# Two scatters a head, squares ahead of rectifications, norms a block later, transposes later, in a fused attention and expert kernel

## The chip, the cores and the metric

The kernel runs on one core of a Trainium2 chip. The metric is the device time of one execution in microseconds (us); the kernel before takes 831.98 us, the median of three runs (830.75 to 832.9).

## What is computed

The reference has two halves, and the second reads what the first wrote.

```python
def _attn_ref(q, k, v, s):            # q, k, v: 8 batches, 8 heads, 576 rows, 64 columns
    scores = scale * np.matmul(q, k.transpose(0, 1, 3, 2))
    bias = -(cum[:, :, :, None] - cum[:, :, None, :])        # cum = cumsum(max(s, 0))
    scores = np.where(causal, -1000000000.0, scores + np.minimum(bias, 0.0))
    attn = softmax(scores)
    return np.matmul(attn, v)
def _moe_ref(x, expert_emb, tau, w1, w2):                    # x: 4608 rows of 512
    logits = normalized(x) @ normalized(expert_emb).T / tau
    expert_idx = np.argmax(logits, axis=1)                   # one of 8 experts a row
    for e in range(E):
        h = np.maximum(x[mask] @ w1[e], 0.0)                 # 512 to 1024
        out[mask] = gate_w[mask, None] * (h @ w2[e])         # 1024 to 512
```

(`softmax` and `normalized` stand for the lines that spell them out.)

## The kernel before

**Attention.** There are 64 heads. `step(n)` (lines 859 to 987) is one step of a software pipeline: for head n the score matmuls and exponentials, for head n - 2 the product with v (`pv`, lines 464 to 482, into the one PSUM tile `om`), for head n - 3 the normalization (`norm1` to `norm3`, VectorE, lines 484 to 510), which writes 72 columns of the row tile `xt` of its batch. `om` must have been read by `norm3` (line 505) before the next `pv` may begin. `pl_` (line 457) makes the low half of the exponentials' split, as a subtraction on GpSimd, or on VectorE.

When the eighth head of a batch is normalized, its 576 rows are routed (`router`): an expert for each row and a place in it. Five scatters of 128 rows (`scat`, line 616, an indirect DMA from GpSimd's queue) then write the rows to `xs` in DRAM, ordered by expert. There are two `xt` tiles, so that the first `norm3` of a batch has to wait until the scatters of the batch two before it have read theirs. How many scatters a step issues is set by `SCN` (line 31), a number for each of a batch's eight heads, up to head 41; from head 42 on (`n < NH - 22` false) it is one a step, and five from head 59 on.

**Experts.** The rows of each expert are gathered back, 128 at a time (`xload`, line 675, at most CAP = 640 rows, so tiles t = 0 to 4). `xprep` transposes them on TensorE (line 700, into a PSUM tile, of which the kind `pxm` exists once and the kind `pxs` twice), copies them as 16 bit values to `xH` (ScalarE, line 705) and the remainder to `xL` (VectorE, line 707); `xstat` squares them (ScalarE, line 689) and sums the expert's logits (VectorE). `l1(m, e, lo, hi)` is block m of eight of the first matrix product (line 788; 12 matmuls where the columns fit in one PSUM bank, else 24), ended by a rectification on ScalarE (line 797, tiles `hv`, `hp`, `hq`) and a subtraction on VectorE (line 798). `l2(e, t)` is the second product for one tile (24 matmuls, line 806), ended by a scaling on VectorE (line 811, into `Kx`) and a scatter to `out` (line 812). Expert 0 is begun with its first SPL = 384 rows while batch 7 is still being routed; tiles 3 and 4 follow.

**Weights.** They come as 32 bit values, 256 KB at a time, into a ring. `wsq` squares them (ScalarE, line 740) and, at the eighth piece, casts the sums (line 742). `wnorm` sums over partitions with a small matmul into `om` (line 751) and makes a power of two of it (VectorE, lines 752 to 758). `wcv` scales and casts a piece (ScalarE, line 768), `wlow` makes its low half (VectorE, line 776) and starts the next load. The first eight pieces lie in tiles that are used again later: `hv` is written over the raw pieces in `vh`, which the `wlow` of those pieces must have read.

All engines run their own queue in the order in which the code issues instructions (`manual_schedule`); nothing reorders them.

Of the kernel before, what the change touches and what calls it, by code (L numbers as in the profile page):

```python
# [31 lines left out]
SCN = [1, 1, 0, 0, 0, 0, 2, 1]  # L32
# [11 lines left out]
SPL = 384  # L44
# [59 lines left out]
def main(ctx, tc, qkh, qkc, vtin, s_in, emb, tau, w1h, w2h, out, shared, nb):  # L104
# [668 lines left out]
    def wlow():  # L773
        while lows:
            q, l, a, s, h = lows.popleft()
            nc.vector.scalar_tensor_tensor(l, a, s, h, op0=ALU.mult, op1=ALU.subtract)  # L776
            wissue(q + 15)
# [19 lines left out]
        nc.scalar.activation(hH, hp, AF.Relu)  # L797
        nc.vector.scalar_tensor_tensor(hL, hp, 0.0, hH, op0=ALU.max, op1=ALU.subtract)  # L798

    def l2(e, t, mid=None):  # L800
        y = pxs()
        for m in range(8):
            wH, wL = wt(2, m)
            hH, hL = htile(m)
            for k, (h, w) in enumerate(((hH, wH), (hL, wH), (hH, wL))):
                nc.tensor.matmul(y, h[:, 128 * t:128 * t + 128], w, start=(m == 0 and k == 0), stop=(m == 7 and k == 2))  # L806
            if m == 3 and mid:
                mid()
        xf = X[("i", e, t)]
        ys = HT["Kx"][:, t % 3]  # L810
        nc.vector.tensor_scalar(ys, y, xf[3], IX["RS"][:, 2 * e + 1:2 * e + 2], op0=ALU.mult, op1=ALU.mult)  # L811
        nc.gpsimd.indirect_dma_start(out=out, out_offset=bass.IndirectOffsetOnAxis(ap=xf[0].bitcast(U32), axis=0),  # L812
                                     in_=ys, in_offset=None, bounds_check=NT - 1, oob_is_err=False)
# [45 lines left out]
    def step(n):  # L859
# [63 lines left out]
        s3(m)  # L923
        if n < 0:
            heat(1)
        wlow()
        if live:
            tbl(n)
        mslot()
        if prev and PS(n) < 1600:  # L930
            pl_(n - 1, PS(n), 1600, "v")
        if n == 1:
            vscale(0)
            fslot()
            while tasks:
                slot()
            emm(0)
            vcp(0, False)
            vcp(0, True)
# [21 lines left out]
        if live:  # L961
            prep(n, False)
            if n:
                vcp(n, True)
        k = n - NH + 8
        if k > 0:
            wsq((0, 2, 3, 6, 8, 8, 9, 10, 12, 14, 16)[k])
            wcv((0, 0, 0, 0, 0, 1, 2, 2, 1, 2, 0)[k], True)
# [7 lines left out]
            loadt(b1, c8)  # L976
        if n == NH - 8:
            wissue(3)
        for _ in range(SCN[c8] if n < NH - 22 else 1 + 4 * (n > NH - 6)):
            scatter()  # L980
        later()
        if live and c == (n < HG):
# [7 lines left out]
    def PS(n):  # L990
        return 1600 if n < NH - 6 else 1024
# [48 lines left out]
    for n in range(1 - LA, NH + 3):  # L1040
        step(n)
    for m in range(3, 8):
        l1(m, 0, 0, SPL, partial(some, 12) if m == 5 else None)
        if m == 3:
            wlow()
            some(12)
            wnorm()
        if m > 3:
            wcv((2, 1, 2, 2)[m - 4])
        if 3 < m < 7:  # L1050
            xstat(0, m - 4)
        if m > 5:
            some(0)
        if m == 7:
            for f in X[("g", 0, 0)][0:2]:
                f()
# [9 lines left out]
        for f in X[("g", 0, 0)][2:4]:  # L1066
            f()

    def second():
        for t in range(SPL // 128, NTL):  # L1070
            xprep(0, t, (pxm, pxs)[t % 2]())
        for t in range(2):
            xload(1, t)
        xprep(1, 2, pxm())

    wsq(18)
    l2(0, 0, opening)
    wsq(21)
    l2(0, 1)
    wsq(24)  # L1080
    l2(0, 2, second)
    for e in range(NE):
        nx = e + 1 < NE
        w2, w1 = 16 * e + 8, 16 * e + 16
        for m in range(8):
            l1(m, e, 0 if e else SPL, CAP)
            if e == 1:
                wsq(w2 + (6, 8)[m] if m < 2 else w1 + (0, 0, 0, 1, 4, 7)[m - 2])
                wcv((2, 0, 2, 2, 2, 2, 0, 0)[m])
                if m == 1:  # L1090
                    wnorm()
            elif e > 1:
                if m < 4:
                    wcv(2)
                elif nx:
                    wsq(w1 + 2 * (m - 3))
            if nx and e > 0 and m == 1:
                xinfo(e + 1, 0, NTL)
            if nx and e > 0 and m == 2:
                for t in range(3):  # L1100
                    xload(e + 1, t)
            if e == 0 and m in (2, 5):
                xprep(1, m // 3, (pxm, pxs)[m // 3]())
                xload(1, 3 + m // 3)
            if e == 0 and m % 2:
                X[("g", 0, SPL // 128)][m // 2]()
            if e > 0 and m < 4:
                X[("g", e, 0)][m]()
            if e == 1 and m == 4:
                count()  # L1110
        for t in range(0 if e else SPL // 128, NTL):
            if nx:
                xprep(e + 1, t, (pxs if e == 0 and t == 3 else pxm)())
                if e and t + 3 < NTL:
                    xload(e + 1, t + 3)
                if e == 0:
                    if t == 3:
                        wnorm()
                    wcv(3)
                    wsq(24 + 2 * (t - 2))  # L1120
                else:
                    if t == 0 and e == 1:
                        wsq(w1 + 8)
                    if t == 1:
                        wnorm()
                    if t:
                        wcv(2)
                    wsq(w2 + 16 + min(8, 2 * t + 2))
                    if t == 4:
                        wnorm()  # L1130
            l2(e, t)

# [120 lines left out]
```

## Time and profile before

| | us |
|---|---|
| median of three runs | 831.98 |
| lowest, highest | 830.75, 832.9 |
| the profiled execution, its own time | 830.1 |
| its span, first to last instruction | 828.3 |
| TensorE busy in the span | 784.2 |
| VectorE, ScalarE, GpSimd busy | 527.5, 570.7, 380.0 |
| mean granted clock of TensorE | 0.979 |

Attention fills the first 370 us of the span, the passage to the experts lies between 330 and 450 us, and the experts fill the rest. Busy shares are averages over all of it. In the rows PE is TensorE's matmuls, PEld its weight loads, DVE VectorE, ACT ScalarE, POOL GpSimd and SP SyncE; a name such as L788 is the line of the kernel.

### The profile page before, as it was taken

Reading aid. Unit: us, or ns where it says so; the run is one execution under the profiler, and the core shown is the slowest. Engines: PE = TensorE matmul, PEld = TensorE weight load, DVE = VectorE, ACT = ScalarE, POOL = GpSimd, SP = SyncE. Lnnn points to the kernel's source line nnn. Section 1 sums busy time; section 2 is a strip of 40 time slices with the busy share of each in tenths; the row PEclk is TensorE's granted clock in tenths of the full one; section 3 lists DMA queues with packets and bytes.
Section 4 is the critical chain, followed back from the end, with each engine's and each line's share of the span. In section 5 each row is a group of like instructions: output and inputs, shape, how many; then the busy total and the mean of one; then the engine's idle time right before and its main releaser. Section 6 shows DMA issues by size and latency. Waiting matters only on the chain. (4 is left out here: it accounts for less than half of the span.)

```text
span 828.3 us, 19525 instructions
## 1 busy us (share of the span) xinstructions
PE 784.2 (95%) x7394; PEld 590.5 (71%) x7394; DVE 527.5 (64%) x1782; ACT 570.7 (69%) x1009; POOL 380.0 (46%) x369
## 2 busy tenths in 40 slices
PE   7699999999999999888898999999999999999992
PEld 3599999999999999874565557466575565655741
DVE  7667888887878777687366555564554556645510
ACT  6589999898989898677355846746557467475400
POOL 8758798989798888552321230221111302211011
PEclk9899999999999999999999999999999999999997
DMA  8977879797979886744333343442553424521010
GB/s 159 204 163 138 184 172 202 178 200 180 201 180 196 185 184 140 230 145 163 110 119 120 123 142 120 140 155 68 155 157 106 143 85 144 179 67 56 1 39 27
DMA packets 44256, 117.17 MB, mean 141 GB/s; under 512 B 6320, under 2 KB 6724, under 8 KB 43294
## 3 DMA queue, kind: packets, MB, share of 16 engines
q0 software_dynamic: 20240, 70.92, 36.6%
q1 hardware_dynamic: 23920, 44.97, 18.1%
q8 instruction: 59, 0.97, 0.5%
q14 instruction: 37, 0.30, 0.1%
HBM read 95.23 MB, written 21.49 MB: 141 GB/s over the span
## 5 line engine op out<-in xcount | busy, mean ns | idle before, releaser
L232 POOL TENSOR_TENSOR PL<-P 128x576 f16<-128x576 f32 (+2 forms) x128 | 202.1, 1673 | 25.8 <-ACT P L452 14.2
L788 PEld LDWEIGHTS <-wt 128*128 128x128 f16 x1536 | 150.3, 98 | 64.4 <-issue 4.2
L788 PE MATMUL h<-xH,wt 128*128 128x320 f16 (+2 forms) x1024 | 188.5, 301 | 0.5 <-DVE hq L798 0.5
L812 POOL DMA_INDIRECT out<-Kx,xj x40 | 39.7, 994 | 182.5 <-DVE Kx L811 178.7
L348 DVE CUSTOM_DVE_ANT_0 junk<-s,mS 128x192 bf16<-128x192 f32 (+3 forms) x256 | 102.1, 420 | 21.4 <-PE s L340 16.8
L480 PE MATMUL om<-vh,P 128*128 128x73 f16 x960 | 110.6, 200 | 4.9 <-DVE xt L505 4.5
L481 PE MATMUL om<-vl,P 128*128 128x72 f16 x960 | 110.1, 198 | 0.0
L482 PE MATMUL om<-vh,PL 128*128 128x73 f16 x960 | 110.0, 199 | 0.0
L679 POOL DMA_INDIRECT Qx<-xs,idx x40 | 42.5, 1062 | 146.3 <-ACT vjunk L689 124.0
L788 PE MATMUL h<-xL,wt 128*128 128x320 f16 (+1 forms) x480 | 106.9, 299 | 0.0
L481 PEld LDWEIGHTS <-P 128*128 128x128 bf16 x960 | 95.2, 99 | 7.3 <-issue 5.8
L340 PE MATMUL s<-qkb 96*128 96x288 f32 (+4 forms) x384 | 95.8, 333 | 3.8 <-DMA qkb<-P 2.7
L806 PE MATMUL pxs<-wt,hp 128*128 128x512 f16 x360 | 97.3, 379 | 0.0
L482 PEld LDWEIGHTS <-PL 128*128 128x128 f16 x960 | 94.4, 98 | 0.0
L480 PEld LDWEIGHTS <-P 128*128 128x128 bf16 x960 | 94.1, 99 | 0.2
L806 PE MATMUL pxs<-wt,hq 128*128 128x512 f16 x360 | 92.0, 383 | 0.0
L811 DVE TENSOR_SCALAR Kx<-pxs,xj,idx 128x512 f32<-128x512 f32 x40 | 32.4, 810 | 81.3 <-PE pxs L806 81.2
L340 PEld LDWEIGHTS s<-qkb 96*128 96x128 f32 x384 | 66.2, 198 | 9.3 <-issue 3.2
L455 ACT ACTIVATE P<-tb 128x1024 f32<-128x1024 f32 x64 | 65.5, 1023 | 7.2 <-PE tb L423 3.6
L806 PEld LDWEIGHTS <-hq 128*128 128x128 f16 x360 | 35.5, 99 | 43.0 <-issue 1.1
L806 PEld LDWEIGHTS <-hp 128*128 128x128 f16 x360 | 35.2, 98 | 42.8 <-issue 0.5
L806 PE MATMUL pxs<-wt,hv 128*128 128x512 f16 x240 | 64.0, 379 | 0.3 <-DVE wt L776 0.3
(223 smaller groups left out, 1722.6 us busy)
## 6 DMA issues: line engine op xcount, KB each, us to landing
qkb<-qkh POOLq DMA_DIRECT2D x15, 1216.0 KB, 9.5
ring<-w2h SPq DMA_DIRECT2D x44, 256.0 KB
ring<-w1h SPq DMA_DIRECT2D x36, 256.0 KB
vT<-vtin SPq DMA_DIRECT2D x28, 320.0 KB
KC<-qkh POOLq DMA_DIRECT2D x15, 576.0 KB, 8.7
QC<-qkh POOLq DMA_DIRECT2D x15, 576.0 KB, 7.7
rw<-w1h SPq DMA_DIRECT2D x15, 256.0 KB
rw<-w2h SPq DMA_DIRECT2D x12, 256.0 KB
```

The lines of the kernel that those rows point to most:

```text
L232: nc.gpsimd.tensor_tensor(out, a, b_, op=ALU.subtract)
L340: nc.tensor.matmul(out, G[g]["QB"][0:96, h, 128 * i:128 * i + 128], G[g]["KB"][0:96, h, lo:hi], start=True, stop=True)
L348: nc.vector.tensor_tensor_reduce(out=jk, in0=src, in1=ms, scale=1.0, scalar=NEG, op0=ALU.add, op1=ALU.max, accum_out=MP[n // 2][:, n % 2, ...
L455: nc.scalar.activation(HD[n]["P32"][:, 576:1600], HD[n]["tb"], AF.Exp, scale=0.125)
L480: nc.tensor.matmul(out, lh, vh[:, kb], start=(kb == 0), stop=False)
L481: nc.tensor.matmul(out[:, u:u + 72], lh, vl[:, kb], start=False, stop=False)
L482: nc.tensor.matmul(out, ll, vh[:, kb], start=False, stop=(kb == j))
L679: ins = nc.gpsimd.indirect_dma_start(out=x.bitcast(I32), out_offset=None, in_=src, in_offset=bass.IndirectOffsetOnAxis(ap=X[("i", e, t)][1 ...
L788: nc.tensor.matmul(h[:, u, 0:b - a], w[:, 128 * c:128 * c + 128], x[:, c, lo + a:lo + b], start=(c == 0 and k == 0), stop=(c == 3 and k == 2))
L806: nc.tensor.matmul(y, h[:, 128 * t:128 * t + 128], w, start=(m == 0 and k == 0), stop=(m == 7 and k == 2))
L811: nc.vector.tensor_scalar(ys, y, xf[3], IX["RS"][:, 2 * e + 1:2 * e + 2], op0=ALU.mult, op1=ALU.mult)
L812: nc.gpsimd.indirect_dma_start(out=out, out_offset=bass.IndirectOffsetOnAxis(ap=xf[0].bitcast(U32), axis=0), in_=ys, in_offset=None, bound ...
```

## The change

Six things are moved; no arithmetic is added or taken away.

- From head 42 on, a head that is the seventh or eighth of its batch issues two scatters in place of one.
- `wlow` stands behind the subtraction `pl_` in a step, and in the three steps that hold blocks 0 to 2 of expert 0 the squares stand ahead of the block.
- The norm of the second matrix of expert 0 stands in the middle of `l1(4)` in place of behind `l1(3)`, and the `xstat` of tiles 0 to 2 a block earlier.
- In `l2(0, 2)` tile 3 is transposed behind m = 4 and tile 4 behind m = 7, in place of both, and a tile of expert 1, behind m = 3. That tile and the next two of expert 1 are transposed behind `l1` blocks 0, 3 and 6 of expert 0, in place of two behind blocks 2 and 5.
- In expert 1 the norm of its second matrix stands behind block 2 in place of block 1, with squares and casts moved to suit; the norm of the next stands at t = 2 in place of t = 1.
- The norm that stood at t = 4 of expert 1 stands behind block 0 of expert 2, with its casts a block later.

```diff
-    def l2(e, t, mid=None):
+    def l2(e, t, mid={}):
...
-            if m == 3 and mid:
-                mid()
+            if m in mid:
+                mid[m]()
...
-        wlow()
         if live:
             tbl(n)
         mslot()
         if prev and PS(n) < 1600:
             pl_(n - 1, PS(n), 1600, "v")
+        wlow()
+        k = n - NH + 8
+        if k > 7:
+            wsq((12, 14, 16)[k - 8])
...
-        for _ in range(SCN[c8] if n < NH - 22 else 1 + 4 * (n > NH - 6)):
+        for _ in range(SCN[c8] if n < NH - 22 else 1 + (c8 > 5) + 4 * (n > NH - 6)):
             scatter()
...
-        l1(m, 0, 0, SPL, partial(some, 12) if m == 5 else None)
+        l1(m, 0, 0, SPL, partial(some, 12) if m == 5 else wnorm if m == 4 else None)
         if m == 3:
             wlow()
             some(12)
-            wnorm()
...
-        if 3 < m < 7:
-            xstat(0, m - 4)
+        if m < 6:
+            xstat(0, m - 3)
...
-    def second():
-        for t in range(SPL // 128, NTL):
-            xprep(0, t, (pxm, pxs)[t % 2]())
-        for t in range(2):
-            xload(1, t)
-        xprep(1, 2, pxm())
+    def third():
+        xprep(0, 3, pxm())
+        xload(1, 0)
+
+    def fourth():
+        xprep(0, 4, pxs())
+        xload(1, 1)
...
-    l2(0, 2, second)
+    l2(0, 2, {4: third, 7: fourth})
...
             if e == 1:
-                wsq(w2 + (6, 8)[m] if m < 2 else w1 + (0, 0, 0, 1, 4, 7)[m - 2])
-                wcv((2, 0, 2, 2, 2, 2, 0, 0)[m])
-                if m == 1:
+                wsq(w2 + (6, 8)[m] if m < 2 else w1 + (0, 0, 0, 0, 1, 4)[m - 2])
+                wcv((2, 0, 0, 2, 2, 2, 2, 0)[m])
+                if m == 2:
                     wnorm()
...
-            if e == 0 and m in (2, 5):
-                xprep(1, m // 3, (pxm, pxs)[m // 3]())
-                xload(1, 3 + m // 3)
+            if e == 0 and m == 0:
+                xprep(1, 2, pxm())
+            if e == 0 and m in (3, 6):
+                xprep(1, m // 3 - 1, (pxm, pxs)[m // 3 - 1]())
+                xload(1, 2 + m // 3)
```

On GpSimd, heads 54 to 58 (the five scatters of batch 5, `xs<-xt`, among the subtractions `PL<-P` and the loads of q and k) stood like this:

```order
L619 DMA xs<-xt,pos 36864x580
L232 TENSOR_TENSOR PL_108<-P_85 128x576
L232 TENSOR_TENSOR PL_108<-P_85 128x1024
L619 DMA xs<-xt,pos 36864x580
L232 TENSOR_TENSOR PL_109<-P_86 128x576
L232 TENSOR_TENSOR PL_109<-P_86 128x1024
L619 DMA xs<-xt,pos 36864x580
L318 DMA KC_91<-qkh 64x4x576
L232 TENSOR_TENSOR PL_110<-P_87 128x576
L232 TENSOR_TENSOR PL_110<-P_87 128x1024
L619 DMA xs<-xt,pos 36864x580
```

The fifth scatter follows six rows further down, behind the copies that end batch 6. Now the same place on GpSimd reads:

```order
L619 DMA xs<-xt,pos 36864x580 x2
L232 TENSOR_TENSOR PL_108<-P_85 128x576
L232 TENSOR_TENSOR PL_108<-P_85 128x1024
L619 DMA xs<-xt,pos 36864x580 x2
L232 TENSOR_TENSOR PL_109<-P_86 128x576
L232 TENSOR_TENSOR PL_109<-P_86 128x1024
L619 DMA xs<-xt,pos 36864x580
L318 DMA KC_91<-qkh 64x4x576
L232 TENSOR_TENSOR PL_110<-P_87 128x576
L232 TENSOR_TENSOR PL_110<-P_87 128x1024
L318 DMA QC_89<-qkh 64x4x576
```

All five are issued by head 56, and no scatter of batch 5 is left in heads 57 and 58; batch 4 has moved in the same way.

On VectorE, step 64 (the normalization `xt<-om,z`, the low halves of two weight pieces that lie in `vh`, the subtraction `PL<-P`, the end of the first expert block `hv`) stood like this:

```order
L505 TENSOR_TENSOR xt<-om,z 128x5x72
L776 SCALAR_TENSOR_TENSOR wt<-vh_106,idx,wt 128x512 x2
L462 TENSOR_TENSOR PL_108<-P_85 128x576
L798 SCALAR_TENSOR_TENSOR hv<-h,hv 128x384
L493 TENSOR_SCALAR z<-om 128x5
```

Now on VectorE:

```order
L505 TENSOR_TENSOR xt<-om,z 128x5x72
L462 TENSOR_TENSOR PL_108<-P_85 128x576
L776 SCALAR_TENSOR_TENSOR wt<-vh_106,idx,wt 128x512 x2
L798 SCALAR_TENSOR_TENSOR hv<-h,hv 128x384
L493 TENSOR_SCALAR z<-om 128x5
```

The two weight instructions now stand right ahead of the end of the block.

On TensorE, in the middle of `l2(0, 2)` (its matmuls `pxs<-wt,...`, and the transposes `<-ident,Qx`, four to a tile) stood:

```order
L806 MATMUL pxs<-wt,hp 128x512
L700 MATMUL pxs<-ident,Qx 128x128 x4
L700 MATMUL pxm<-ident,Qx 128x128 x8
L806 LDWEIGHTS hq
L806 MATMUL pxs<-wt,hq 128x512
```

Now on TensorE, the last rows of `l2(0, 2)` and the first of the block behind it:

```order
L806 LDWEIGHTS hv
L806 MATMUL pxs<-wt,hv 128x512
L700 MATMUL pxs<-ident,Qx 128x128 x4
L788 LDWEIGHTS wt
L788 MATMUL h<-xH,wt 128x256
```

Four of the twelve transposes stand at the end of `l2(0, 2)`, four earlier in it behind m = 4, and four behind the first block that follows.

## Rows read from the trace of the kernel before

**Rows 1.** Windows: start:end, length, busy (instructions) by engine, clock, DMA share, GB/s

```profile
85.00:290.00 205.00, 205.00 (x2956) 200.43 (x2955) 166.15 (x709) 189.16 (x243) 175.43 (x148) 1.00 0.85 188
446.00:815.00 369.00, 367.32 (x2243) 220.28 (x2241) 195.31 (x471) 209.07 (x471) 63.17 (x63) 1.00 0.34 109
```

**Rows 2.** Timeline, TensorE: start, length, instruction, [idle before <- releaser]

```profile
295.23 0.19 PE L480 MATMUL om<-vh,P 128*128 128x73 f16 x1 [0.51 <-DVE xt L505]
336.00 0.73 PE L279 MATMUL V<-en,vT 128*128 128x144 f32 x4 [0.62 <-DVE vl L290]
339.01 0.22 PE L480 MATMUL om<-vh,P 128*128 128x73 f16 x1 [2.27 <-DVE xt L505]
376.70 0.18 PE L751 MATMUL om<-idx,onesb 128*128 128x8 bf16 x1 [2.09 <-DVE oh L573]
401.86 0.66 PE L700 MATMUL pxm<-ident,Qx 128*128 128x128 f32 x4 [2.04 <-DMA Qx<-xs,idx]
403.92 1.11 PE L700 MATMUL pxm<-ident,Qx 128*128 128x128 f32 x4 [1.40 <-DVE xL L707]
440.72 0.17 PE L751 MATMUL om<-idx,onesb 128*128 128x8 bf16 x1 [2.73 <-ACT idx L742]
```

**Rows 3.** Windows behind three of those waits

```profile
339.00:342.50 3.50, 3.49 (x49) 3.43 (x49) 1.61 (x5) 0.51 (x2) 0.00 (x0) 0.53 0.02 5
404.00:407.50 3.50, 3.50 (x11) 1.77 (x12) 0.88 (x3) 0.59 (x1) 2.89 (x3) 0.55 0.37 101
441.30:444.80 3.50, 3.50 (x16) 2.01 (x14) 2.23 (x13) 0.00 (x0) 0.00 (x0) 0.51 0.05 19
```

**Rows 4.** Timeline, steps 58 and 59: GpSimd, ScalarE, VectorE

```profile
330.88 1.01 POOL L619 DMA_INDIRECT xs<-xt,pos  x1 [0.54 <-issue]
331.84 2.11 POOL L232 TENSOR_TENSOR PL<-P 128x576 f16<-128x576 f32 x2
331.80 1.02 ACT L455 ACTIVATE P<-tb 128x1024 f32<-128x1024 f32 x1
331.69 2.88 DVE L462 TENSOR_TENSOR PL<-P 128x576 f16<-128x576 f32 x1
338.42 0.53 DVE L505 TENSOR_TENSOR xt<-om,z 128x360 f32<-128x360 f32 x1 [1.38 <-DMA xs<-xt,pos]
```

**Rows 5.** Timeline, GpSimd: a pair of scatters in an earlier batch

```profile
106.38 1.13 POOL L619 DMA_INDIRECT xs<-xt,pos  x1 [0.61 <-DVE z L493]
107.82 1.03 POOL L619 DMA_INDIRECT xs<-xt,pos  x1 [0.30 <-issue]
```

**Rows 6.** Timeline, step 64: VectorE, ScalarE

```profile
363.52 3.41 DVE L776 SCALAR_TENSOR_TENSOR wt<-vh,idx,wt 128x512 f16<-128x512 f32 x2
366.85 0.75 DVE L462 TENSOR_TENSOR PL<-P 128x576 f16<-128x576 f32 x1
367.02 0.49 ACT L797 ACTIVATE hv<-h 128x384 f16<-128x384 f32 x1 [3.01 <-DVE wt L776]
```

**Rows 7.** Windows, one line's instructions alone: start:end, length, PE, PEld, clock, DMA, GB/s

```profile
447.00:457.00 10.00, 10.00 (x76) 7.18 (x74) 1.00 0.44 137
391.00:396.00 5.00, 5.00 (x24) 2.24 (x23) 1.00 0.52 196
```

**Rows 8.** Timeline, ScalarE and VectorE on tile 4 of expert 0

```profile
401.90 0.63 ACT L689 ACTIVATE vjunk<-Qx 128x512 bf16<-128x512 f32 x1 [1.45 <-DMA Qx<-xs,idx]
403.17 0.69 DVE L707 TENSOR_TENSOR xL<-pxm,xH 128x512 f16<-128x512 f32 x1 [0.92 <-ACT xH L705]
```

**Rows 9.** A gather's issue, its transposes, and the landing time of all 40 gathers

```profile
405.26 1.03 POOL L679 DMA_INDIRECT Qx<-xs,idx  x1 [0.30 <-PE pxm L700]
412.51 0.60 PE L700 MATMUL pxm<-ident,Qx 128*128 128x128 f32 x4
DMA to landing us min/median/max: 3.4/3.7/6.7
```

**Rows 10.** Timeline, ScalarE: the cast that ends the squares, expert 1

```profile
440.47 0.20 ACT L742 CAST idx<-idx 128x8 bf16<-128x8 f32 x1
```

More of the change, by code (lines that the diff above doesn't have):

```diff
@@ L964, in step @@
                 vcp(n, True)
-        k = n - NH + 8
         if k > 0:
@@ L1067, in opening @@
             f()
-    def second():
-        for t in range(SPL // 128, NTL):
-            xprep(0, t, (pxm, pxs)[t % 2]())
-        for t in range(2):
-            xload(1, t)
-        xprep(1, 2, pxm())
+    def third():
[4 more added lines that the diff above has]
+        xload(1, 1)
     wsq(18)
-    l2(0, 0, opening)
+    l2(0, 0, {3: opening})
     wsq(21)
@@ L1087, in main @@
             if e == 1:
-                wsq(w2 + (6, 8)[m] if m < 2 else w1 + (0, 0, 0, 1, 4, 7)[m - 2])
-                wcv((2, 0, 2, 2, 2, 2, 0, 0)[m])
-                if m == 1:
+                wsq(w2 + (6, 8)[m] if m < 2 else w1 + (0, 0, 0, 0, 1, 4)[m - 2])
+                wcv((2, 0, 0, 2, 2, 2, 2, 0)[m])
+                if m == 2:
                     wnorm()
             elif e > 1:
-                if m < 4:
+                if e == 2 and m == 0:
+                    wsq(w2 + 8)
+                    wnorm()
+                if e == 2 and m < 5:
+                    wcv(2 if m else 0)
+                if e > 2 and m < 4:
                     wcv(2)
-                elif nx:
+                if nx and m > 3:
                     wsq(w1 + 2 * (m - 3))
@@ L1121, in main @@
                 else:
-                    if t == 0 and e == 1:
-                        wsq(w1 + 8)
-                    if t == 1:
+                    if e == 1 and t < 2:
+                        wsq(w1 + 6 + 2 * t)
+                    if t == 1 + (e == 1):
                         wnorm()
                     if t:
-                        wcv(2)
-                    wsq(w2 + 16 + min(8, 2 * t + 2))
-                    if t == 4:
+                        wcv(2 if e > 1 else (0, 0, 3, 3, 2)[t])
+                    if e > 1 or t > 1:
+                        wsq(w2 + 16 + min(8, 2 * t + 2 if e > 1 else 3 * t - 4))
+                    if t == 4 and e > 1:
                         wnorm()
```

## The prediction

> **What bounds the kernel now.** I read the windows first, by stage. TensorE is busy without a gap in most of the attention, 205.00 of 205 us, and again from 446 us to the end, where the 1.7 us that are missing lie behind its last matmul [rows 1]. What is moved in those stretches saves time only if TensorE waits there, and it does not. So the gain has to come from the passage between them. There I read the timeline of TensorE for waits, each with what ended it [rows 2]: 0.51 us at 295, 0.62 and 2.27 at 336 to 339, 2.09 at 376.70, 2.04 and 1.40 at 402 to 404, 2.73 at 440.72, together 11.7 us. Last I read the granted clock behind them [rows 3]. Behind three of the places it is 0.53, 0.55 and 0.51 over 3.5 us: most of that time it is at the lower of its two levels, 1.2 in place of 2.4 GHz. TensorE works through all three windows, so the time lost is (1 - clock) x 3.5 us: 1.65, 1.6 and 1.7. Ahead of the first fall TensorE stood for 0.62 and 2.27 us with 0.7 us of work between, ahead of the second for 2.04 and 1.40, ahead of the third for 2.73. Behind the single 2.09 it did not fall. Waits and slow stretches make 16.7 us; the change touches each of them.
>
> **The change part by part.**
>
> *Scatters two a head.* At 339.01 TensorE waits for the normalization of batch 7's first head, line 505, and that one for a scatter: the last of batch 5, issued at 330.88, is released at 338.42, 7.5 us later [rows 2, 4]. In the new order batch 5 is done at head 56, two heads of some 5 us earlier, and 7.5 us of landing are over by then. VectorE's own 1.38 us of waiting go for certain. More may go: the scatter of 330.88 held GpSimd up, whose two subtractions then ran to 333.95, and VectorE's subtraction, 0.75 us long when GpSimd is idle [rows 6], took 2.88 us beside them [rows 4]. Without the scatter GpSimd's first subtraction can end before the second has its input (the exponential ends at 332.82), and VectorE's can be done in that gap, near 332.6 in place of 334.57. Then the chain up to line 505 is 2 us earlier and both waits (2.27 and 0.62, the latter for VectorE too) are gone: 2.9 us. The lower bound is 1.4. I take 2.5, nearer to the upper, since the second subtraction cannot begin earlier than 332.82. The clock has then no cause to fall: 1.65 us more.
>
> The row of the 2.88 us shows an instruction with two inputs in SBUF stopped through two of GpSimd's, though it began 0.15 us ahead of them. The Trainium skill (SBUF — State Buffer, Who interferes with whom) has it that whoever issues first gets the shared ports and the other blocks for the whole instruction. The trace agrees on the blocking, not on who was first; by the rule the gap would go to VectorE and the term would be 2.9, by the row alone (blocked through both subtractions again) 1.4.
>
> What the moved scatters cost: GpSimd issues one more in heads 46, 47, 54 and 55, 1.0 us and a 0.3 us gap each [rows 5], and fewer later. It is idle for 29.6 of 205 us [rows 1], about 0.7 us a head, so it runs up to 1.2 us late for two heads; its product is used a head later. A pair at 106.38 and 107.82 already runs so in a stretch in which TensorE never waits [rows 1, 5]. I set this at nothing; if that cover were gone it would be 1.2 us twice. The same edit moves batch 4's scatters, and the 0.51 us wait at 295.23 is of the same kind (first head of batch 6): 0.5, at least 0.
>
> *Behind the subtraction, and the norm half a block later.* In step 64 VectorE's two weight instructions end at 366.93, ScalarE's rectification follows at 367.02, and while it runs VectorE does the subtraction of 0.75 us [rows 6]. In the new order that subtraction stands ahead, so the rectification, VectorE's end of the block, the normalization behind it and TensorE's next `pv` all come 0.67 us later. The squares ahead of the rectifications hide: ScalarE had been waiting 3.01 us there. Against that the norm of line 751 lets six matmuls of `l1(4)` go first. A block's matmul takes 10/74 = 0.135 us for 320 columns [rows 7], so 0.16 for 384, and six are 0.97 us out of the wait of 2.09. Net 0.3 us gained; between 0.7 lost and 1.0 gained. The wait that stays is about 1.1 us, for the same routing instruction.
>
> *Transposes later.* Tile 3's transposes ended at 401.86 - 2.04 = 399.8 [rows 2], so the twelve matmuls of `l2(0, 2)` ahead of them had ended near 399.1. In the new order three more go ahead of tile 3 and nine more ahead of tile 4, 5/23 = 0.217 us each [rows 7]: 399.1 + 12 x 0.217 + 0.45 for the first four transposes is 402.1, and tile 4's gather has landed at 401.86. The third set of transposes (1.40 us wait for the single `pxm` tile) goes behind a block, where that tile is free. What is late next: the block behind `l2(0, 2)` needs tile 4's `xH` and `xL`, and no work is left ahead of it. From the landing at 401.90 to the end of line 707, 403.17 + 0.69, are 2.0 us [rows 8]; the transposes take 0.45 of them, so TensorE waits 1.5 us where nothing waited. 3.4 less 1.5 gives 1.9, with the clock's 1.6 together 3.5; between 1.9 (the clock falls all the same) and 4.2.
>
> *Gathers of expert 1.* A gather was issued at 405.26 and used at 412.51, 7.2 us later [rows 9]. The issue hangs on GpSimd's queue and stays where it is, while TensorE comes some 3.5 us earlier: 3.7 us remain for a landing time of 3.4 to 6.7, median 3.7. Two gathers stand like this. I take 0.2 us of new waiting; 0 to 3.
>
> *The norm of expert 1 a block later.* TensorE waited 2.73 us until 440.72 for ScalarE's cast of 440.47, which ends at 440.67 [rows 2, 10]. One block of 24 matmuls, 24 x 0.135 = 3.2 us, now goes first: it would reach the norm at 438.0 + 3.2 = 441.2, 0.5 us behind the cast. The squares ahead of that cast keep their places. Gain 2.7, and the clock's 1.7. The casts that wait for the norm come a block later too, and behind them on ScalarE stand the rectifications of blocks 3 to 6; but the last of these eight pieces is cast behind block 6, a whole block ahead of the first `l2` that reads any. The norms moved to t = 2 and into expert 2 lie in the full stretch [rows 1]: nothing to gain, and nothing to lose as long as their casts are done 5 us ahead, which they are.
>
> The sum: 2.5 + 1.65 + 0.5 + 0.3 + 3.5 - 0.2 + 2.7 + 1.7 = 12.65 us. The profiled execution took 830.1 us, 1.8 more than its span of 828.3; it would take 817.4, and the median of 831.98 becomes **819.3**.
>
> **The rivals.**
>
> *The clock falls once all the same.* For it: 1.5 us of waiting before the new block at 402, and step 64's wait grows by 0.67 us, while it is not known how little standing is enough. Against it: a single 2.09 did not do it. One fall costs 1.65: 821.0.
>
> *The scatter isn't what is waited for.* The releasers are inferred; if the 7.5 us have another cause, the terms 2.5, 1.65 and 0.5 go: 824.0. Against it: line 505 waits for nothing else that is late, and earlier batches, whose scatters end a head sooner, show no wait [rows 1].
>
> *The late transposes cost what they save.* If tile 4 lands late, or its copies queue, the 1.5 us become 3.4 and the clock falls: 3.5 lost, 822.8.
>
> *Slower: scatters that wait for each other.* If the second of a pair could only be issued once the first has landed (7.5 us, [rows 4]), each pair would hold GpSimd 8.5 us. Two pairs follow each other, 17 us, of which the free time and the head of lead cover some 7: TensorE waits 10 us in each of two batches, with a slow stretch each (3.3), and the scatter terms (4.65) are not gained: 819.3 + 4.65 + 20 + 3.3 = 847. It decides the sign from about 3.5 us a pair on. Against it: the pair of [rows 5] is issued 0.3 us apart.
>
> **How the numbers follow.** Forecast 0.62; clock 0.18; scatter not the cause 0.07; transposes 0.09; slower 0.04. Runs of this kernel tell about 0.3% (2.5 us) from no change. All cases but the last are faster by more than that, except for a sum of mishaps to which I give 0.02: faster 0.94, same 0.02, slower 0.04. The range: below, the upper ends of the terms (2.9, 1.0, 4.2, no new wait) give 2.0 us more and the runs spread by 1 us: 816. Above, it takes in one fall of the clock, the failed transposes, and the gathers' wait short of its end: 824.
>
> **What would show it.** Right: no scatter wait on line 505 and a clock of 1.0 behind 336 us; a wait of about 1.5 us ahead of the first 256 column block; none on line 751 in expert 1, and a clock of 1.0 there; step 64's `pv` wait longer. Wrong: a clock at the lower level in any of the three places, a wait on line 700 for gathers of expert 1, GpSimd's subtractions ending a `pv` wait in heads 46 to 57.

## The result, and the profile after

The changed kernel takes 821.56 us (median of four runs, 817.95 to 823.24) against 832.25 us before (830.75 to 832.9): a ratio of 0.9872, 95% interval 0.9834 to 0.9911. It is faster, and inside the range (816 to 824). The forecast was 819.3. In a second group of runs the ratio was 0.9901 (0.987 to 0.9932). The profiled execution took 820.65 us, its span is 818.9, TensorE is busy for 782.7 of it (784.2 before) at a mean clock of 0.983.

Medians hide where the time went, and so does the span: every profile of this program, changed or not, begins with some 50 us that vary (last section). So I compare starts of the same instruction in two profiles, less the same difference at line 505 of head 30, in the even stretch (202.59 us in the profile of before). For a block it is the start of its rectification. This is how far the changed kernel is **ahead** (us):

| at the start of | ahead |
|---|---|
| line 505 of head 48 (step 51) | 0.4 |
| line 505 of head 58 (step 61) | 4.8 |
| first rectification, `l1(0)` (step 64) | 2.5 |
| third, `l1(2)` (step 66) | 0.8 |
| fifth, `l1(4)`, behind the second matrix's norm | 1.9 |
| first of the 256 column blocks | 6.9 |
| first block of expert 1 | 4.7 |
| third of expert 1, behind its norm | 9.3 |
| last | 9.2 |

TensorE's waits in the passage, from the timeline of the changed kernel (start, length, instruction, [idle before <- releaser]), answer [rows 2]:

```profile
360.40 0.19 PE L480 MATMUL om<-vh,P 128*128 128x73 f16 x1 [0.74 <-DVE xt L505]
366.51 0.19 PE L480 MATMUL om<-vh,P 128*128 128x73 f16 x1 [2.50 <-DVE xt L505]
375.72 0.18 PE L751 MATMUL om<-idx,onesb 128*128 128x8 bf16 x1 [1.03 <-DVE oh L573]
401.07 0.27 PE L788 MATMUL h<-xH,wt 128*128 128x256 f16 x1 [0.67 <-ACT xH L705]
401.80 0.27 PE L788 MATMUL h<-xL,wt 128*128 128x256 f16 x1 [0.46 <-DVE xL L707]
408.33 0.27 PE L788 MATMUL h<-xH,wt 128*128 128x256 f16 x1 [0.29 <-DVE hq L798]
412.04 0.27 PE L788 MATMUL h<-xH,wt 128*128 128x256 f16 x1 [0.93 <-DVE hq L798]
```

The 0.51, 0.62, 2.27, 2.04, 1.40 and 2.73 us of [rows 2] are gone, and the 2.09 is 1.03. New are 1.13 us ahead of the first 256 column block and 1.22 in the blocks behind it. The wait in step 65 has grown to 2.50; before it was 1.75, a wait that is not among [rows 2]:

```profile
369.02 0.20 PE L480 MATMUL om<-vh,P 128*128 128x73 f16 x1 [1.75 <-DVE xt L505]
```

The windows behind step 59, step 65, `l2(0, 2)` and expert 1's norm answer [rows 3]; the clock stands behind the five busy times:

```profile
335.50:339.00 3.50, 3.43 (x60) 3.27 (x58) 3.36 (x10) 3.44 (x9) 2.40 (x2) 1.00 0.04 9
367.20:370.70 3.50, 3.50 (x37) 2.44 (x34) 2.34 (x6) 2.92 (x8) 0.00 (x0) 0.52 0.00 0
401.00:404.50 3.50, 2.98 (x26) 2.57 (x26) 2.15 (x6) 1.33 (x5) 2.17 (x3) 1.00 0.19 75
433.00:436.50 3.50, 3.50 (x29) 2.55 (x27) 3.08 (x10) 2.86 (x9) 0.00 (x0) 1.00 0.74 238
```

The three falls of before are gone; a new one stands behind step 65 and costs 1.6 us (from 2.5 ahead to 0.8).

Steps 58 and 59, GpSimd and VectorE, answer [rows 4]. No scatter stands there, VectorE's subtraction fits between GpSimd's two and takes 0.75 in place of 2.88 us, and line 505 starts at 335.10 in place of 338.42 without a wait:

```profile
330.41 1.15 POOL L232 TENSOR_TENSOR PL<-P 128x576 f16<-128x576 f32 x1 [1.54 <-ACT P L452]
331.44 0.75 DVE L462 TENSOR_TENSOR PL<-P 128x576 f16<-128x576 f32 x1
332.64 0.94 POOL L232 TENSOR_TENSOR PL<-P 128x448 f16<-128x448 f32 x1 [1.08 <-ACT P L455]
335.10 0.53 DVE L505 TENSOR_TENSOR xt<-om,z 128x360 f32<-128x360 f32 x1
```

Steps 62 to 64, GpSimd, VectorE, ScalarE, answer [rows 6]. GpSimd issues batch 6's five scatters (the first and the last are shown), then runs four subtractions; VectorE's, now first, is stopped beside them for 2.84 us, and ScalarE's rectification waits 3.07:

```profile
351.84 1.47 POOL L619 DMA_INDIRECT xs<-xt,pos  x1 [3.87 <-DVE xt L505]
357.50 0.93 POOL L619 DMA_INDIRECT xs<-xt,pos  x1 [0.30 <-issue]
358.42 4.05 POOL L232 TENSOR_TENSOR PL<-P 128x576 f16<-128x576 f32 x4
360.26 2.84 DVE L462 TENSOR_TENSOR PL<-P 128x576 f16<-128x576 f32 x1
363.02 1.40 DVE L776 SCALAR_TENSOR_TENSOR wt<-vh,idx,wt 128x512 f16<-128x512 f32 x2
364.52 0.49 ACT L797 ACTIVATE hv<-h 128x384 f16<-128x384 f32 x1 [3.07 <-DVE wt L776]
```

The first scatter's wait of 3.87 us is put down to line 505, which is inferred. The semaphores in the trace tell it otherwise. The positions, line 601, are written by 347.5. What comes last are the landings of expert 0's first three gathers, which read the `xs` that the scatters write. The third of them, in the profile of before and in this one:

```profile
349.67 1.01 POOL L679 DMA_INDIRECT Qx<-xs,idx  x1 [0.30 <-issue]
344.89 1.01 POOL L679 DMA_INDIRECT Qx<-xs,idx  x1 [0.30 <-issue]
```

It lands at 354.63 and 350.94, and the first scatter goes out 0.89 and 0.90 us behind that (355.52 and 351.84). It does so 0.89 or 0.90 us behind that landing in all eleven profiles that have the five scatters in a row there.

### The profile page after: what moved, and what is told of

It reads as the page before. It is cut to its first block, busy times and chain, and to the rows that moved or that the text cites. A ratio compares the mean times of both kernels' runs of the same rounds, so it can differ in the third digit from the quotient of the medians.

```text
span 818.9 us, 19526 instructions
## 1 busy us (share of the span) xinstructions
PE 782.7 (96%) x7394; PEld 590.0 (72%) x7394; DVE 525.9 (64%) x1782; ACT 570.8 (70%) x1009; POOL 380.2 (46%) x369
## 5 line engine op out<-in xcount | busy, mean ns | idle before, releaser
L232 POOL TENSOR_TENSOR PL<-P 128x576 f16<-128x576 f32 (+2 forms) x128 | 203.3, 1687 | 24.1 <-ACT P L455 11.6
```

Source lines behind the costliest of these rows:

```text
L232: nc.gpsimd.tensor_tensor(out, a, b_, op=ALU.subtract)
```

## The experiments

The table has the ratio to the kernel before, and how far each profile is ahead at five of the places above. The ratios come from groups of runs with a kernel before of their own: a_scat1, a_wlow0, a_norm1 and a_trans0; after_again, b_scat2, a_gate and a_late6; before_again, a_wlow0_gate and a_late6_gate_wlow0; and a_spread6_gate_wlow0 alone. By these medians only b_scat2 is clear of both groups of the changed kernel. What each move is worth is therefore read from the profiles, one for each edit.

| run | median us | ratio, interval | head 58 | `l1(0)` | `l1(4)` | first of expert 1 | last |
|---|---|---|---|---|---|---|---|
| changed, first profile | 821.56 | 0.9872, 0.9834-0.9911 | 4.8 | 2.5 | 1.9 | 4.7 | 9.2 |
| after_again | 822.35 | 0.9901, 0.987-0.9932 | 4.2 | 1.9 | 1.4 | 4.2 | 8.8 |
| before_again | 833.22 (one) | | 2.8 | 1.5 | 0.0 | 0.2 | 0.2 |
| a_scat1 | 823.11 | 0.992, 0.9893-0.9948 | 2.9 | 0.8 | 1.9 | 4.8 | 9.4 |
| b_scat2 | 828.24 | 0.9987, 0.9962-1.0013 | 4.4 | 2.8 | 2.8 | 3.0 | 3.0 |
| a_wlow0 | 818.68 | 0.9862, 0.9813-0.9912 | 4.4 | 3.0 | 4.1 | 7.0 | 11.6 |
| a_norm1 | 824.89 | 0.9937, 0.9911-0.9963 | 5.4 | 3.4 | 2.8 | 5.7 | 5.8 |
| a_trans0 | 823.53 | 0.9916, 0.9891-0.9941 | 5.5 | 4.0 | 5.1 | 5.2 | 9.8 |
| a_gate | 820.85 | 0.9885, 0.983-0.9939 | 4.5 | 2.5 | 2.8 | 6.2 | 10.8 |
| a_late6 | 819.68 | 0.9894, 0.9833-0.9955 | 4.2 | 4.1 | 3.6 | 6.3 | 10.9 |
| a_wlow0_gate | 819.71 | 0.9854, 0.9815-0.9893 | 4.5 | 2.9 | 3.9 | 7.4 | 12.0 |
| a_late6_gate_wlow0 | 822.93 | 0.9879, 0.9841-0.9916 | 4.4 | 4.6 | 1.4 | 4.7 | 9.3 |
| a_spread6_gate_wlow0 | 816.98 | 0.9822, 0.9792-0.9852 | 4.5 | 3.8 | 3.7 | 7.6 | 12.1 |

**The two kernels once more** (no edit).

> The kernel before itself, for a second profile of it. What comes with the order of the instructions is the same as in its first profile: VectorE's subtraction of 2.9 us at step 58, 2.09 us on line 751, 2.73 us in expert 1, 1.71 us in step 65. What is chance differs: the scatter of step 58 was released 7.5 us after its issue in the first profile and 1.38 us of line 505's wait hung on that; in the run with one scatter a head it was there in time. If its landing is chance, line 505 waits for VectorE alone here, TensorE's wait at step 59 is 1.0 in place of 2.27 us and the clock may stay at 1.00; if it is the rule, the rows repeat.

> The changed kernel itself, for a second profile of it beside the runs of this group. What comes with the order of the instructions has to be the same as in its first profile: no wait of line 505 for a scatter at step 59, TensorE's wait of 2.5 to 2.6 us in step 65, 0.67 and 0.46 us ahead of the first block of 256 columns. What differs is chance: where the clock falls in the second profile as in the first, behind the wait of step 65, it comes with the order; where it stays at 1.00, the wait lies at the edge of it.

Steps 58 and 59 in the second profile of before, TensorE, VectorE and GpSimd:

```profile
339.77 0.73 PE L279 MATMUL V<-en,vT 128*128 128x144 f32 x4 [0.62 <-DVE vl L290]
341.47 0.19 PE L480 MATMUL om<-vh,P 128*128 128x73 f16 x1 [0.98 <-DVE xt L505]
335.45 2.88 DVE L462 TENSOR_TENSOR PL<-P 128x576 f16<-128x576 f32 x1
340.88 0.53 DVE L505 TENSOR_TENSOR xt<-om,z 128x360 f32<-128x360 f32 x1
334.64 1.01 POOL L619 DMA_INDIRECT xs<-xt,pos  x1 [0.53 <-issue]
```

VectorE's 2.88 us repeats; the wait for the scatter doesn't. It was there within 340.88 - 334.64 = 6.2 us, in the first profile [rows 4] only after 7.5. TensorE waits 0.98 in place of 2.27, the clock stays up, and this profile of before is 2.8 us ahead of the other by step 61. It loses that again by step 66, by a fall of the clock and a standing of three engines that the last section tells of. So of what I read in [rows 2 to 4] as one stall, the 1.38 us of landing and the fall of 1.65 were chance. In a_scat1, too, the scatter landed sooner: 5.4 us behind its start, against 7.4 in the first profile of before.

The second profile of the changed kernel repeats step 59 without a wait, 2.33 us in step 65 with a fall of the clock, and 0.67, 0.46, 0.28 and 0.93 behind `l2(0, 2)`.

**One scatter a head again (a_scat1), and two a head alone (b_scat2).**

```diff
-        for _ in range(SCN[c8] if n < NH - 22 else 1 + (c8 > 5) + 4 * (n > NH - 6)):
+        for _ in range(SCN[c8] if n < NH - 22 else 1 + 4 * (n > NH - 6)):
```

> The changed kernel with one scatter a head from head 42 on, as before; the other five moves stay. Theory (line 505 waits for the scatter of two batches ago, and the paired scatters took that wait away): the normalization of batch 7's first head starts 4.3 to 4.8 us later, with VectorE's subtraction again near 2.9 us, TensorE's wait of 0.5 us near 295 back and a granted clock near 0.53 behind 339 us; time 821.6 + 4.8 = 826.4. Rival (the scatter is not what is waited for; something else of the change made steps 58 and 59 early): 821.6, and steps 58 and 59 as in the changed kernel. Where the clock does not fall: 824.7.

> The kernel before with the two scatters a head alone. Theory (GpSimd, held up by the scatter in step 58, stops VectorE's subtraction, and line 505 waits for that scatter to land): at step 59 VectorE's subtraction takes 0.75 us, neither wait is left, and from step 48 to step 59 the kernel is 2.7 (where only GpSimd was in the way) to 4.6 us (where the landing and the clock come on top, as in the profile of before) ahead of the kernel before; behind that 65 it gives some back, since in before's order TensorE waits 1.71 us there; time 0.9970 to 0.9945 of before. Rival (paired scatters delay GpSimd as much as they save): within 0.5 us of before at step 59.

Between heads 48 and 58, a_scat1 gains 2.8 us on the first profile of before and the changed kernel 4.4: undoing the edit costs 1.6. VectorE's subtraction is 2.88 us long again, the wait is 0.98, and no scatter is late; the clock stays up, so the 4.3 to 4.8 us of the theory did not come:

```profile
335.65 2.88 DVE L462 TENSOR_TENSOR PL<-P 128x576 f16<-128x576 f32 x1
341.67 0.20 PE L480 MATMUL om<-vh,P 128*128 128x73 f16 x1 [0.98 <-DVE xt L505]
```

b_scat2 gains 4.3 us there on the first profile of before and 1.5 on the second. Both rivals fall, and the price has two parts: 1.5 to 1.6 us in both pairs, from GpSimd stopping VectorE, and up to 2.8 more where the scatter lands late and the clock falls. By the medians the edit alone is not told from no change (0.9987). In the changed kernel little of it may last: from the third rectification on a_scat1 is as far ahead as the changed kernel (0.8 at both, 9.4 and 9.2 at the end), for in its profile the clock did not fall in step 65, behind a wait of 2.61 us.

**The low halves first again (a_wlow0).** The call of `wlow()` moves back ahead of `tbl(n)`.

```diff
+        wlow()
         if live:
             tbl(n)
...
             pl_(n - 1, PS(n), 1600, "v")
-        wlow()
```

> The changed kernel with the low halves of the weights again ahead of the subtraction in a step; the squares stay ahead of the blocks. Theory (the new order on VectorE alone makes TensorE's wait of 2.50 us in step 65, and the clock falls behind that wait): the first rectification comes 0.7 us earlier, the wait is 1.7 to 1.8, the clock stays at 1.00: 821.6 - 2.3 = 819.3. First rival (TensorE stood too long in steps 63 to 65 in any case, since the late start near 356 us comes with the earlier arrival there): the wait is 0.7 us shorter, the clock falls all the same: 820.9. Second rival (what is won in step 64 is given back at the second matrix's norm, which waits for routing on VectorE): 821.6.

```profile
358.07 4.76 DVE L776 SCALAR_TENSOR_TENSOR wt<-vh,idx,wt 128x512 f16<-128x512 f32 x2
357.56 4.05 POOL L232 TENSOR_TENSOR PL<-P 128x576 f16<-128x576 f32 x4
364.92 0.20 PE L480 MATMUL om<-vh,P 128*128 128x73 f16 x1 [1.88 <-DVE xt L505]
```

TensorE's wait is 1.88 us, 0.5 to 0.7 less than the 2.33 to 2.61 of five profiles with the new order, and the clock stays up, near the theory's numbers. In two of those five (a_scat1 and a_trans0) it stays up as well, so that the order alone does not decide the fall. Ahead of what is left of the wait stands GpSimd: its four subtractions behind the five scatters, which end at 361.6, stop VectorE's first weight instruction, and `pv` itself waits for them twice (0.36 and 0.51 us, released by `PL` of line 232).

**Expert 1's norm behind block 1 again (a_norm1).**

```diff
-                wsq(w2 + (6, 8)[m] if m < 2 else w1 + (0, 0, 0, 0, 1, 4)[m - 2])
-                wcv((2, 0, 0, 2, 2, 2, 2, 0)[m])
-                if m == 2:
+                wsq(w2 + (6, 8)[m] if m < 2 else w1 + (0, 0, 0, 1, 4, 7)[m - 2])
+                wcv((2, 0, 2, 2, 2, 2, 0, 0)[m])
+                if m == 1:
```

> The changed kernel with the norm of expert 1's second matrix again behind block 1, and its squares and casts as before. Theory (TensorE waits for ScalarE's last cast and the clock falls behind that): wait of 2.7 us on line 751 in expert 1 and a granted clock near 0.51 behind it, time 821.6 + 4.4 = 826.0. Rival (TensorE now comes to expert 1 some 4.7 us earlier and without low clock, so ScalarE is as early too and the wait is smaller than before, without a fall of the clock): 822 to 824.

```profile
436.11 0.17 PE L751 MATMUL om<-idx,onesb 128*128 128x8 bf16 x1 [2.73 <-ACT idx L742]
```

The wait is back to the hundredth, with the clock at 0.52 from 436 to 439.5 us; from expert 1's first block to its third a_norm1 gains 0.1, the changed kernel and every other one that keeps the move 4.6. The theory holds. The median points the same way (0.9937), but its interval touches one of the changed kernel's and overlaps the other.

**All twelve transposes behind m = 3 again (a_trans0).**

```diff
-    l2(0, 2, {4: third, 7: fourth})
+    l2(0, 2, {3: second})
...
-            if e == 0 and m == 0:
-                xprep(1, 2, pxm())
-            if e == 0 and m in (3, 6):
-                xprep(1, m // 3 - 1, (pxm, pxs)[m // 3 - 1]())
-                xload(1, 2 + m // 3)
+            if e == 0 and m in (2, 5):
+                xprep(1, m // 3, (pxm, pxs)[m // 3]())
+                xload(1, 3 + m // 3)
```

> The changed kernel with all twelve transposes again behind m = 3 of l2(0, 2), and two tiles of expert 1 behind blocks 2 and 5. Theory (TensorE waits there for tile 4's gather and for the single tile pxm, with a fall of the clock): waits of about 2.0 and 1.4 us and a granted clock near 0.55 behind them, no wait at the first block of 256 columns, time 821.6 + 2.8 = 824.4. Rival (the late transposes only move the wait: what they save at 402 us is given back in the blocks behind): 821.6 to 822.4.

```profile
399.25 0.66 PE L700 MATMUL pxm<-ident,Qx 128*128 128x128 f32 x4 [2.11 <-DMA Qx<-xs,idx]
401.31 0.90 PE L700 MATMUL pxm<-ident,Qx 128*128 128x128 f32 x3 [1.40 <-DVE xL L707]
```

Both waits are back, the clock falls with the second (0.51 from 400.7 to 404.2), and from `l1(7)` to the first block of expert 1 it gains 0.1 us where the changed kernel gains 2.8. The theory holds to the size.

**The gate of expert 0's last tiles later (a_gate).** Nine small instructions on VectorE behind block 3 of 256 columns, and four behind block 7, go to where VectorE has time.

```diff
-            if e == 0 and m % 2:
-                X[("g", 0, SPL // 128)][m // 2]()
+            if e == 0 and m == 7:
+                X[("g", 0, SPL // 128)][0]()
...
                     wsq(24 + 2 * (t - 2))
+                    if t == 3:
+                        for f in X[("g", 0, SPL // 128)][1:]:
+                            f()
```

> The changed kernel with the gate of expert 0's last two tiles (nine small instructions on VectorE behind block 3, and four behind block 7) moved behind the casts of the second product's first tile, where VectorE has time. Theory (the block behind them waits for VectorE's end of a block, which stands behind those nine): TensorE's wait of 0.9 to 1.3 us for hq goes, and expert 1 begins 1.2 us earlier: 820.4. Rival (the wait is made by ScalarE's late rectifications): the wait stays within 0.3 us of what it was, 821.6. A cost that would show: VectorE's scaling at the end of the second product's first tile comes later and the product after next waits for it.

In the changed kernel VectorE goes through the nine from 409.82 (the first and the last are shown) and only then ends two blocks; TensorE's 0.93 us of above wait for that:

```profile
409.82 0.16 DVE L83 RECIPROCAL idx<-idx 128x2 f32<-128x2 f32 x1
411.48 0.17 DVE L91 TENSOR_TENSOR xj<-xj,idx 128x16 f32<-128x16 f32 x1
411.57 0.75 DVE L798 SCALAR_TENSOR_TENSOR hq<-h,hq 128x256 f16<-128x256 f32 x2
```

With the move only 0.27 us is left, and the stretch from the first 256 column block to expert 1 costs 1.2 us in place of 2.1 to 2.2. So the theory names the 0.93 us; the 0.27 stays, and its cause stays open. Nothing later waits for the moved instructions.

a_wlow0_gate joins this move with a_wlow0 and comes out near what was expected: 12.0 us ahead at the end (12.3), a wait of 1.66 us in step 65 (1.9), no fall of the clock between 60 us and the last expert, and 0.9854 of before.

**GpSimd's scatters of batch 6 in step 64 (a_late6), with the two moves of above (a_late6_gate_wlow0), or spread (a_spread6_gate_wlow0).**

```diff
-        for _ in range(SCN[c8] if n < NH - 22 else 1 + (c8 > 5) + 4 * (n > NH - 6)):
+        for _ in range(SCN[c8] if n < NH - 22 else 1 + (c8 > 5) + 4 * (n > NH - 6) if n < NH - 2 else 5 * (n >= NH)):
```

and in the spread one

```diff
+        for _ in range(SCN[c8] if n < NH - 22 else (0, 2, 5)[n - NH + 2] if NH - 3 < n < NH + 1 else 1 + (c8 > 5) + 4 * (n > NH - 6)):
```

> The changed kernel with the five scatters of batch 6 issued in step 64, behind GpSimd's last four subtractions, in place of ahead of them in step 62. Theory (what is lost in steps 63 to 65 is lost to GpSimd: its five scatters, 1.3 us each, stand ahead of the subtractions that pv and VectorE wait for): TensorE's waits for PL in step 64 go, VectorE's subtraction there takes 0.75 in place of 2.84 us, the wait of 2.5 us in step 65 falls below 0.8 and the clock does not fall; from step 61 to the first rectification nothing is lost in place of 2.05 us, and with what before lost there too some 3 us are won: 818.5. Rival (VectorE's two weight instructions and ScalarE's squares are what comes last there): the wait in step 65 stays over 1.5 us, 821.

> The changed kernel with the low halves of the weights again ahead of the subtraction in a step, and the gate of expert 0's last two tiles moved behind the casts of the second product's first tile. Theory (both moves are worth what they were apart: 0.7 us of waiting in step 65, with it the clock, and 0.7 to 1.0 us in the blocks of expert 0): counted from the even stretch of attention the last expert block is 12.3 us ahead of the kernel before, against 8.8 to 9.2 of the changed kernel; the wait in step 65 is 1.9 us, the clock falls nowhere between 60 and 800 us; time 0.985 to 0.986 of before. Rival (the clock falls in step 65 all the same, as it does behind 2.3 to 2.6 us): 1.6 us less.

> The three moves together: the low halves ahead of the subtraction, the gate later, and the scatters of batch 6 in step 64 behind GpSimd's last subtractions. Theory (GpSimd's five scatters ahead of its subtractions bound steps 62 to 65): VectorE's first weight instruction of step 64 is no longer stopped through four of GpSimd's (4.76 us for the two with the low halves first), no pv waits for PL in step 64, the wait in step 65 is under 1.0 us, and the first rectification is 4.5 to 5.4 us ahead of the kernel before where it is 2.4 to 3.0 in the changed kernel; the last expert block is 13 to 14 us ahead; time 0.984 of before. Rival (what is won there is taken back a few us later by what all engines wait for, as the 1.58 and 0.40 us that the move alone showed): the first rectification ahead by 4.5 us, the third by 3 only, and the end no better than with the other two moves.

> As the last kernel, but the five scatters of batch 6 are spread: none in step 62, two in step 63 ahead of one of GpSimd's subtractions, three in step 64 behind the last. In the runs so far TensorE, VectorE and ScalarE all stood together for up to 3 us some 4 to 5 us behind the first of the five, at 356 where they went out in step 62, at 367 where they went out in step 64; nothing that the profile shows ended it. Theory (five in a row in front of a queue make it): spread, the three engines do not stand together for 0.5 us or more between 350 and 372 us, no pv waits for PL, the first rectification is 4.4 us or more ahead of the kernel before and the third still 4 us, the last expert block 13 us; time 0.984 of before. Rival (they stand whenever these scatters go out while weights are loaded, whatever the grouping): a standing of over 0.5 us 4 to 5 us behind the first or the third of them, and the last block is 9 to 12 us ahead.

a_late6, VectorE and TensorE:

```profile
361.67 0.75 DVE L462 TENSOR_TENSOR PL<-P 128x576 f16<-128x576 f32 x1
362.33 1.41 DVE L776 SCALAR_TENSOR_TENSOR wt<-vh,idx,wt 128x512 f16<-128x512 f32 x2
354.78 2.30 DVE L776 SCALAR_TENSOR_TENSOR wt<-rw,idx,wt 128x512 f16<-128x512 f32 x2
357.74 0.66 PE L700 MATMUL pxs<-ident,Qx 128*128 128x128 f32 x4 [1.58 <-DVE wt L707]
366.58 0.20 PE L480 MATMUL om<-vh,P 128*128 128x73 f16 x1 [1.17 <-DVE xt L505]
```

Without scatters ahead of them, GpSimd's subtractions are over in time, VectorE's two rows of step 64 have their bare lengths, and the first rectification is 4.1 us ahead in place of 1.9 to 2.5: GpSimd's queue was the bound. The wait in step 65 is 1.17 us, where the theory had under 0.8, and the clock stays up. Not all of the gain stays. GpSimd's subtractions now fall on the pair of weight instructions a step earlier (2.30 in place of 1.41 us); the 1.58 us that TensorE waits for that are covered by the first rectification's own slack. But 1.5 us are lost by the third, around which ScalarE and VectorE stand idle for 1.50 and 1.13 us with "remote" and "issue" as releaser. With all three moves together more of it is lost:

```profile
368.39 0.17 DVE L493 TENSOR_SCALAR z<-om 128x5 f32<-128x5 f32 x1 [2.61 <-remote]
369.94 0.49 ACT L797 ACTIVATE hp<-h 128x384 f16<-128x384 f32 x1 [2.76 <-remote]
369.40 0.19 PE L480 MATMUL om<-vh,P 128*128 128x73 f16 x1 [2.70 <-DVE xt L505]
366.83 0.99 POOL L619 DMA_INDIRECT xs<-xt,pos  x1 [0.30 <-issue]
```

The first rectification is 4.6 us ahead, the third 0.4: three engines stand together while GpSimd issues scatters, and the clock falls behind that. The rival's picture holds here, and more was taken back than it had (the third at 3). Spread (two in step 63, three in step 64), the engines don't stand together, but VectorE's weight pair of step 63 takes 2.80 us. The first of the two takes 0.78 us beside a scatter, near its bare 0.74; the second, begun at 354.55, ends behind a subtraction that GpSimd ran from 354.91 to 356.09:

```profile
353.84 2.80 DVE L776 SCALAR_TENSOR_TENSOR wt<-rw,idx,wt 128x512 f16<-128x512 f32 x2
357.97 1.11 PE L700 MATMUL pxs<-ident,Qx 128*128 128x128 f32 x4 [2.11 <-DVE wt L707]
367.26 0.20 PE L480 MATMUL om<-vh,P 128*128 128x73 f16 x1 [0.71 <-DVE xt L505]
```

Its profile has a fall of the clock behind the 2.11 us. The first and third rectifications are 3.8 and 2.7 us ahead, where the theory wanted 4.4 and 4, and the end 12.1, 0.9 short of it. It is the fastest of all: 816.98 us, 0.9822 (0.9792 to 0.9852). That is clearly below the kernel before. Its interval stays below that of the changed kernel's second group and overlaps the first's by 0.0018. Against a_wlow0_gate (0.9854) it is not decided.

## Why the prediction was right, and where it was not

*Sign and range* came out, since all but one of the terms came with their sign. By the first profile the kernel gained 9.2 us where the sum said 12.65; the 3.4 us that are missing lie in two places.

*Scatters: mechanism right, size by luck.* 4.15 us and the 0.5 near 295 were forecast; the first profiles show 4.8 by head 58. I weighed GpSimd's block against the landing and took 2.5 for the two waits; the rows gave 2.89, the upper bound. The Trainium skill (SBUF — State Buffer, Who interferes with whom) says that whoever issues first keeps the other out for its whole instruction. The forecast by that rule, 2.9, was the better one here: VectorE's subtraction, begun at 331.44, ran bare before GpSimd's second began at 332.64. Step 64 goes against the rule: VectorE's, begun at 360.26, ended at 363.10, behind two of GpSimd's that began after it (360.42 and 361.53, the last until 362.48). The term itself took one trace for what the program always does. With a second profile of before it would have been 1.6, for the landing and the fall were chance. The 0.5 near 295 isn't shown: at head 48 the profiles with paired scatters lie between 0.2 us behind and 1.0 ahead. Paired scatters cost nothing that shows there: the rival that they wait for each other is out.

*Step 64 and the norm: this step failed.* "Net 0.3 us gained" came out as 2.9 lost, from 4.8 ahead at head 58 to 1.9 at `l1(4)`. Its parts were right: the order lengthens TensorE's wait by 0.5 to 0.7 (forecast 0.67), the norm half a block later gains 0.97 in every profile that has it and nothing in b_scat2, which has not (0.97), and 1.03 us of the wait stays (1.1). What I left out is what comes next when TensorE reaches step 62 some 4.7 us early. GpSimd can't: its five scatters wait for expert 0's third gather to land. That was issued 4.8 us earlier than before, but took 6.05 us to land in place of 4.96 (5.0 to 6.4 over these profiles), so that the scatters went out only 3.7 us earlier (351.84 against 355.52) and the four subtractions behind them ended 3.2 us earlier. 3.2 less the 0.7 of the order are the 2.5 us ahead at the first rectification: 2.3 were lost on the way from head 58. I had written that the moved scatters delay nothing, and never looked at the five that weren't moved. a_late6 shows it: with them out of the way this place costs 0.2 in place of 2.3.

*The clock.* Behind the longer wait of step 65 it fell, for 1.6 us. That was my first rival, with a chance of 0.18 and 821.0 us, and it is what happened in both profiles of the changed kernel. That the median, 821.56, is near 821.0 is in part luck, for the fall is only 1.6 of the 3.4 us that are missing. I gave the rival too little. The wait grew about as priced (to 2.50 and 2.33 us), but I had not read that it started from 1.75, so that some 2.4 us were due, more than the single 2.09 that I held against the fall.

*Transposes: 2.8 in place of 3.5.* The new wait is 1.13 us (forecast 1.5) and the clock stays up, as forecast. What I missed stands behind it. The blocks of 256 columns now follow each other with nothing else late, so VectorE's nine small instructions between two of them come last: 0.93 and 0.29 us. I had costed the moves into these blocks at nothing and named no cover for them. a_gate shows it for the 0.93. The wait for gathers of expert 1 (0.2) did not come.

*Norm of expert 1: 4.6 against 4.4.* The wait, the fall of the clock, and the absence of a cost for the later casts are as forecast, and the best part of the gain. The squares ahead of the rectifications and the moves into expert 2 were not undone by themselves; from the third block of expert 1 to the end nothing is gained or lost (9.3 to 9.2).

## What to carry to other kernels

When an edit lets one engine arrive several microseconds earlier at a busy place, read there the queue of every engine that was *not* edited: the one that can't come as much earlier, here GpSimd, whose five scatters wait for a gather to land, is the new bound. Look behind the releaser that a row names, too: it is inferred, and here it was another. A stall of one trace that hangs on a DMA's landing should be priced from two profiles, since its landing and the fall of the clock behind it may both be chance. To size an edit of 1 us in a program whose runs differ by several, compare the same instruction's start in two profiles, counted from a stretch that the edit doesn't touch.

## What the runs showed of the hardware

**The start varies more than most edits are worth.** Line 505 of head 30, far ahead of anything that was changed, starts between 201.53 us (a_wlow0) and 207.62 (a_gate); in the two profiles of the changed kernel at 202.55 and 206.77, in those of before at 202.59 and 206.36. From there to head 44 all profiles agree to 0.05 us. The late ones are, in the main, those in which the last stretch of TensorE at its lower clock ahead of that place ends late (at 45.4 us in the first profile of before, at 49.2 in the second; 44.4 in a_wlow0, 51.9 in a_gate).

**The clock falls by chance behind waits of middle length.** After one wait of TensorE of 2.70 to 2.77 us it fell in 5 of 5 places; of 2.33 to 2.61 in 3 of 5, with the same instructions around it; of 2.09 or 2.10 in 0 of 3, yet once behind 2.11 elsewhere. With waits close together that end in 1.40 at `l2(0, 2)` it fell in 4 of 4. It also fell behind the 2.27 us of [rows 2], with 0.62 shortly ahead, and twice just behind the standings of the next paragraph, where the longest single wait was 1.20 and 1.85. A fall cost 1.6 us.

**TensorE, VectorE and ScalarE sometimes stand together.** In five of the fourteen profiles (both kernels among them) all three are idle at once somewhere in steps 63 to 66, for 0.5 to 1.8 us in all and at most 1.2 at a stretch (not up to 3, as I wrote ahead of the spread run), while GpSimd issues scatters or just behind that; most in a_gate and in the second profile of before. The releaser reads "issue" or "remote". In a_late6_gate_wlow0, where the scatters went out later, the standing came later too; with the scatters spread it did not show in the one profile there is. No packet of an instruction queue starts in those stretches in any of the five. What ends it is not in the profile, and stays open.
